# Attention and two expert layers on one core: weighted sums with both halves of V in one product, and what moves with them

## The chip, the cores and the metric

The kernel runs on one core of a Trainium2 chip. Its engines are TensorE (PE), VectorE (DVE), ScalarE (ACT), GpSimd (POOL) and SyncE (SP), which issues the DMAs. Each works through its own instructions in order and waits on semaphores for the others. The metric is the device time of one execution in microseconds (us), the median of several.

## The reference

```python
scores = scale * np.matmul(q, k.transpose(0, 1, 3, 2))          # 4 batches, 8 heads, 576 x 64
kth = np.partition(scores, -32, axis=-1)[..., -32:-31]
scores = np.where(scores >= kth, scores, -1e9)
attn = np.exp(scores - np.max(scores, axis=-1, keepdims=True))
attn = attn / (np.sum(attn, axis=-1, keepdims=True) + 1e-09)
x = (attn @ v) as (2304, 512)
h = x @ w_in                                                     # 512 -> 1024
solu = h * softmax(h)
ln = (solu - mean) / np.sqrt(var + 1e-06) * g_ln
x2 = ln @ w_out                                                  # 1024 -> 512
h = x2 @ w_in2                                                   # 512 -> 2048
out = (h * (1 / (1 + np.exp(-1.702 * h)))) @ w_out2              # 2048 -> 512
```

All of it is float32.

## The kernel before

Products are made in half precision, with each operand as a high half and a low half (`split`): the high half is the number rounded, the low half the rest, and a product is three products, high by high, high by low and low by high. `split` is used for keys, queries, values and weights. In its most frequent form ScalarE scales the raw tile, then squares it with the sum kept (`total`), then writes the high half, and GpSimd writes the low half; the Square writes its unneeded values into the tile of the high half.

**Attention.** Queries are taken in blocks of 128 rows; the last 64 rows of a batch form a block of last rows (`r == NEWT`). A block has four steps (two for last rows), each with two heads: 72 steps. A step goes through TensorE scores (L455), ScalarE copy, VectorE `fold` (L473, L474) and top-k rounds (L484, L487), GpSimd `pick`, ScalarE and GpSimd `mask` (L505), ScalarE `exp_of`, whose accumulator gives the row sums `rsum`, the two halves `high` and `low` (L523), and a DMA transpose `turn` (L528). Three steps behind, `back` (L606) multiplies the transposed weights `et` by V and sums up in the PSUM tile `av`, one bank, of which there is one. For each head and each of five chunks of keys there are three products of 64 columns. When a block is complete, `finish` calls `evac_main` (or `evac_tail`): `recip` (L628, L629) makes the reciprocals of the row sums, and L644 (or L668) multiplies `av` by them into `x`.

**The expert layers.** Each block of 128 rows of `x` then goes through `Block`: `a` (L709), `top`, `e1`, `solu`, `z_high`, `z_low`, `b` (L776), then four times `c` (L806), `tanh`, `gelu` (L815), `g_high`, `g_low` (L826), `d` (L833), and `store`. Its parts are placed between the parts of the attention steps by `at`, some steps later. Weights are decoded from their 64-bit form on VectorE (L249 to L254) and split in the first steps.

**The check at the end.** The program keeps sums of squares, picks and, in `ysum`, the row sums of each stored `y`. At the end VectorE compares them with bounds (`inside`, L1110 to L1113), a product with ones (L1129) adds up the rows, and the flag (L1131) is loaded by every engine; if it is set, a slower version of the whole computation follows.

**What sets the order.** The code is written in the order of the steps, and a scheduler reorders it at build time by priorities and its own estimate. Each engine's order is fixed after that.

Of the kernel before, what the change touches and what calls it, by code (L numbers as in the profile page):

```python
# [41 lines left out]
W_CHECK = 60  # L42
PIN_TO = -1
# [5 lines left out]
S_X2 = 2.0 ** 6  # L49
# [31 lines left out]
def layers(ctx, tc, quick, q, k, v, w1, w2, g_ln, w3, w4, out):  # L81
# [24 lines left out]
    if quick:  # L106
# [5 lines left out]
        ysum = cst.tile([128, NBLK], F32, name="ysum")  # L112
        for i, x in enumerate((1.0, -S_EXP, BIG)):
            nc.vector.memset(pickc[:, :, i], x)
        ones = cst.tile([128, 128], F32, name="ones")
# [4 lines left out]
    def split(raw, hi, lo, scale, what, total=None):  # L120

        n = lo_n[what] = lo_n.get(what, -1) + 1
        how = LO[what][n % len(LO[what])]
# [20 lines left out]
    one = ctx.enter_context(tc.tile_pool(name="one", bufs=1))  # L144
    ep = ctx.enter_context(tc.tile_pool(name="ep", bufs=R_BUFS if quick else 2))
# [43 lines left out]
    nc.vector.memset(mhalf, -0.5)  # L189
    wraw = {}  # L190
# [433 lines left out]
    xm = {}  # L624

    def recip(r, n):

        nc.vector.scalar_tensor_tensor(r[:, 0:n], r[:, 0:n], 1e-9, r[:, 0:n], op0=ALU.add, op1=ALU.max)  # L628
        nc.vector.reciprocal(r, r)  # L629

    def evac_main(blk):
        b, r = blk
        if r == 0:
            batch_coef(b)
        recip(rsum[blk], 8)
        if quick:
            rr = rsum[blk].rearrange("p (a c) -> p a c", c=2)
        else:
            rr = sm.tile([128, 4, 2], F32, tag="rr", name="rr")
            iv = bsc[b][:, 1, 1, :]  # L640
            nc.vector.scalar_tensor_tensor(rr, rsum[blk].rearrange("p (a c) -> p a c", c=2), bcf[b][:, 1:2],
                                           iv[:, :, None].to_broadcast([128, 4, 2]), op0=ALU.mult, op1=ALU.mult)
# [5 lines left out]
        return x, None if quick else bcf[b][:, 2:3]  # L648

    def evac_tail(blk):  # L650
# [5 lines left out]
        if b not in bcf:  # L656
            batch_coef(b)
        rs = rsum[blk][:, 0:4]
        recip(rs, 4)
        rr = rs.rearrange("p (a c) -> p a c", c=2) if quick else sm.tile([128, 2, 2], F32, tag="rrt", name="rrt")  # L660
        for z in range(0 if quick else 2):
            rows = slice(64 * z, 64 * z + 64)
            iv = bsc[b][rows, 1, 1, z::2]
            nc.vector.scalar_tensor_tensor(rr[rows], rs[rows].rearrange("p (a c) -> p a c", c=2),
                                           bcf[b][rows, 1:2], iv[:, :, None].to_broadcast([64, 2, 2]),
                                           op0=ALU.mult, op1=ALU.mult)
        xt = one.tile([128, 512], F32, tag="x", name="xtl")[:, 0:256].rearrange("p (h d) -> p h d", d=64)
        nc.vector.tensor_tensor(xt, pav[blk][:, 0:256].rearrange("p (h d) -> p h d", d=64),  # L668
                                rr.rearrange("p a c -> p (a c)")[:, :, None].to_broadcast([128, 4, 64]),
                                op=ALU.mult)  # L670
# [25 lines left out]
    class Block:  # L696
# [121 lines left out]
        def g_high(self, g):  # L818
# [3 lines left out]
            act(gh[:, 0], t.rearrange("p (a n) -> p a n", a=4))  # L822
# [13 lines left out]
        def store(self):  # L836
            y = at.tile([128, 512], F32, tag="t", name="y")
            if quick:
# [324 lines left out]
```

## Time and profile before

| | |
|---|---|
| median of 3 timed runs | 961.12 us (960.68 to 962.55) |
| the profiled execution, its own time | 967.89 us |
| its span | 966.0 us |
| TensorE busy | 766.2 us (79%) |
| VectorE busy | 766.7 us (79%) |
| ScalarE busy | 722.9 us (75%) |
| GpSimd busy | 695.9 us (72%) |

The span is from the first to the last instruction of the profiled execution; its own time is 1.9 us longer. Busy time is a share of the whole span; stretches differ, and a table by stretches shows them apart. In rows, PE is TensorE, PEld its weight loads, DVE VectorE, ACT ScalarE, POOL GpSimd and SPq the DMA issues of SyncE. L160 is the line of a helper through which all ScalarE operations go.

### The profile page before, as it was taken

What the parts mean: (1) busy time and instruction counts of PE and PEld (TensorE: products, weight loads), DVE (VectorE), ACT (ScalarE), POOL (GpSimd) and SP (SyncE); (2) the same over time, 40 slices, a digit from 0 to 9 for tenths busy, and PEclk for the clock granted to TensorE, in tenths of its full rate; (3) what the DMA queues carried; (4) which work ended last, traced back from release to release, by engine and by line L of the source; (5) the groups of instructions that cost most, each with busy time, mean ns of one, the idle gap of its engine ahead of it and who ended that gap; (6) DMA issues with size and microseconds to landing.
All of it is one profiled execution on the core that took longest, in us unless ns stands there. A gap on an engine that the chain in (4) does not pass through costs nothing.

```text
span 966.0 us, 22236 instructions
## 1 busy us (share of the span) xinstructions
PE 766.2 (79%) x8228; PEld 497.6 (52%) x8228; DVE 766.7 (79%) x2150; ACT 722.9 (75%) x1257; POOL 695.9 (72%) x699
## 2 busy tenths in 40 slices
PE   1122524566688899989999899898999899999996
PEld 0011211534355556656665666565665666666564
DVE  4999999988698999897889988887988899511221
ACT  4689898587888978778899877778997878834431
POOL 2488999778968788777899886777987777733311
PEclk9995756677899999999999999998999899999998
DMA  6998666556757767566778577568756745532200
GB/s 159 314 308 202 178 164 151 122 117 126 143 122 139 122 119 136 105 119 124 137 138 156 115 127 118 100 111 150 137 113 116 130 76 90 97 69 45 44 14 25
DMA packets 337733, 122.66 MB, mean 127 GB/s; under 512 B 315344, under 2 KB 329168, under 8 KB 337616
## 3 DMA queue, kind: packets, MB, share of 16 engines
q1 hardware_dynamic: 337616, 121.16, 61.7%
q8 instruction: 66, 1.08, 0.5%
q14 instruction: 51, 0.42, 0.1%
HBM read 39.85 MB, written 4.72 MB: 46 GB/s over the span
## 4 chain that ended last, share of the span: by engine, by line
PE 26%; ACT 16%; DVE 16%; DMA 15%; POOL 14%; issue 8%; SPq 4%; ACTq 0%; POOLq 0%; DVEq 0%
PE h L806 9%; PE o L833 7%; ACT s L160 4%; PE x L776 4%; DVE wk L484 4%; POOL eh L523 4%; DVE wk L487 4%; PE ha L709 3%; POOL s L505 3%; POOL wt L138 2%; PE sc L455 2%; DMA kt<-kq 2%; ACT kq L160 2%; DMA qt<-kq 2%; DMA et<-eh 2%
## 5 line engine op out<-in xcount | busy, mean ns | idle before, releaser
L484 DVE MAX8 wk<-wk 128x8 f32<-128x296 f32 x576 | 242.2, 461 | 0.0
L806 PE MATMUL h<-x2t,wt 128*128 128x128 f16 x3456 | 217.1, 225 | 20.1 <-DVE t L815 14.8
L806 PEld LDWEIGHTS <-wt 128*128 128x128 f16 x3456 | 206.8, 101 | 27.2 <-issue 15.7
L833 PE MATMUL o<-wt,gh 128*128 128x512 f16 x864 | 203.3, 385 | 9.7 <-DVE wt L254 7.6
L523 POOL TENSOR_TENSOR eh<-s,eh 128x576 f16<-128x576 f32 x144 | 181.5, 1283 | 38.8 <-ACT eh L160 26.2
L505 POOL TENSOR_TENSOR s<-s,r 128x576 f32<-128x576 f32 x144 | 181.8, 1283 | 34.7 <-ACT r L160 34.5
L487 DVE MATCH_REPLACE8 wk<-wk 128x296 f32<-128x296 f32 x432 | 193.6, 458 | 0.0
L455 PE MATMUL sc<-kt,qt 128*128 128x64 f16 (+7 forms) x640 | 99.3, 321 | 71.7 <-DMA qt<-kq 30.8
L606 PE MATMUL av<-vt,et 128*128 128x64 f16 (+1 forms) x2400 | 90.1, 201 | 60.7 <-DMA et<-eh 52.2
L833 PEld LDWEIGHTS <-gh 128*128 128x128 f16 x864 | 83.8, 99 | 105.0 <-issue 16.1
L826 POOL TENSOR_TENSOR gh<-t,gh 128x512 f16<-128x512 f32 x72 | 83.6, 1161 | 73.2 <-ACT gh L160 73.1
L160 ACT ACTIVATE s<-s,picks 128x576 f32<-128x576 f32 x144 | 110.4, 768 | 16.9 <-POOL s L505 16.5
L606 PEld LDWEIGHTS <-et 128*128 128x128 f16 (+1 forms) x2400 | 82.2, 106 | 72.9 <-DMA et<-eh 55.9
L776 PE MATMUL x<-wt,zt 128*128 128x512 f16 x432 | 105.4, 397 | 14.3 <-DMA zt<-zh 14.2
L709 PE MATMUL ha<-wt,xt 128*128 128x512 f16 x432 | 101.9, 394 | 14.5 <-DMA xt<-xhl 11.1
L455 PEld LDWEIGHTS <-qt 128*128 128x128 f16 (+1 forms) x640 | 49.5, 110 | 123.5 <-DMA qt<-kq 31.2
L815 DVE SCALAR_TENSOR_TENSOR t<-t,h 128x512 f32<-128x512 f32 x72 | 49.2, 683 | 76.3 <-ACT t L160 73.3
L160 ACT ACTIVATE r<-s,picks 128x576 bf16<-128x576 f32 x144 | 103.5, 766 | 5.5 <-POOL picks L497 5.4
L160 ACT ACTIVATE t<-h 128x512 f32<-128x512 f32 x72 | 42.3, 588 | 70.7 <-PE h L806 61.9
L160 ACT ACTIVATE s<-sc 128x1152 f32<-128x1152 f32 x72 | 80.7, 1120 | 14.5 <-PE sc L455 8.5
L160 ACT ACTIVATE wt<-wt 128x512 f16<-128x512 f32 (+1 forms) x115 | 68.0, 627 | 22.9 <-DVE wt L254 10.5
L160 ACT ACTIVATE eh<-s 128x1152 f16<-128x1152 f32 x72 | 83.3, 1156 | 0.7
(84 smaller groups left out, 1070.1 us busy)
## 6 DMA issues: line engine op xcount, KB each, us to landing
wt<-in_moe_w_in_dram SPq DMA_DIRECT2D x24, 512.0 KB, 4.8
wt<-in_moe_w_out_dram SPq DMA_DIRECT2D x24, 512.0 KB, 5.7
qt<-qt SPq DMA_DIRECT2D x72, 64.0 KB, 2.0
raw<-in_k_dram SPq DMA_DIRECT2D x32, 128.0 KB, 2.5
raw<-in_q_dram SPq DMA_DIRECT2D x16, 256.0 KB, 3.3
vraw<-in_v_dram SPq DMA_DIRECT2D x32, 128.0 KB, 2.4
out_dram<-y SPq DMA_DIRECT2D x16, 256.0 KB, 3.2
et<-eh SPq DMA_TRANSPOSE x72, 4.7
```

The source lines that it names most:

```text
L160: nc.scalar.activation(out, in_, func, **kw)
L455: nc.tensor.matmul(sc[rows, i * S + c0:i * S + c1], t[qi // 4][:, hl, qi % 4, rows], kts[kp][:, k0 + c0:k0 + c1], start=(hl == 0), stop=(h ...
L484: nc.vector.max(out=wk[:, i, at_:at_ + 8], in_=wk[:, i, 0:W_END])
L487: nc.vector.match_replace(out=wk[:, i, 0:W_END], in_to_replace=wk[:, i, at_:at_ + 8], in_values=wk[:, i, 0:W_END], imm_value=LOW)
L505: nc.gpsimd.tensor_tensor(s[:, i], s[:, i], r[i], op=ALU.subtract)
L523: nc.gpsimd.tensor_tensor(eh[:, 1, cols], s[:, i], eh[:, 0, cols], op=ALU.subtract)
L606: nc.tensor.matmul(o[rows, col:col + 64], et[:, ea, 4 * i + c, rows], vts[kp][:, va, vc:vc + 64], start=(n == 0), stop=(n == 14))
L709: nc.tensor.matmul(h[:, half * 512:half * 512 + 512], self.xt[:, a, kc], w1v(kc, w, half), start=(n == 0), stop=(n == 11))
L776: nc.tensor.matmul(self.x2, self.zt[:, a, kc], w2v(kc, w), start=(n == 0), stop=(n == 23))
L806: nc.tensor.matmul(h2[:, mm * 128:(mm + 1) * 128], w3v(kc, w, 4 * g + mm), self.x2t[:, a, kc], start=(n == 0), stop=(n == 11))
L826: nc.gpsimd.tensor_tensor(gh[:, 1], t.rearrange("p (a n) -> p a n", a=4), gh[:, 0], op=ALU.subtract)
L833: nc.tensor.matmul(self.o, gh[:, a, mm], w4v(4 * g + mm, w), start=(g == 0 and n == 0), stop=(g == 3 and n == 11))
```

## The change

`back` takes both halves of V as one moving operand: for each chunk the high half of the weights is multiplied by 128 columns (V's high half and, 640 elements further, its low half), and the low half of the weights by 64 columns, added to the first 64. Four heads of 128 columns fill the bank, so after every second step `weighted` takes the sums out: the row sums get 1e-9 on GpSimd, VectorE makes the reciprocals and multiplies the two halves apart (L657, L659), and GpSimd adds them (L660). `x` has a pool of its own. In `split` the Square is written behind the halves and into a tile of its own; one Square of a single column stands at the start. The load of `gl` is issued after the first loads. For the last block the check takes, in place of the sums of `y`, the sums of the gelu tile's high half (`accum_out` in `g_high`) and its maximum, and `y` is stored without a sum.

```diff
@@ split
         if how == "A" and scale is not None:
             act(raw, raw, AF.Copy, scale=scale)
-            if total is not None:
-                act(hi, raw, AF.Square, scale=1.0 / scale, accum_out=total)
+            back = 1.0 / scale if total is not None else 1.0
             scale = None
-        elif total is not None:
-            act(hi, raw, AF.Square, accum_out=total)
...
+        if total is not None:
+            junk = squares[:, 0:raw.shape[1] * raw.shape[2]].rearrange("p (c d) -> p c d", d=raw.shape[2]) if len(raw.shape) == 3 \
+                else squares[:, 0:raw.shape[1]]
+            act(junk, raw, AF.Square, scale=back, accum_out=total)
         return how
...
     nc.vector.memset(mhalf, -0.5)
+    if quick:
+        act(squares[:, 0:1], mhalf, AF.Square)
@@ back
-        if j == 0:
+        if j == 0 or quick and j == 2:
             pav[blk] = p_av.tile([128, 512], F32, tag="av", name="av")
         o = pav[blk]
+        for i in range(2 if quick else 0):
+            hs = heads(blk, j, i)
+            col = hs[0][1] % 4 * 128
+            for c in range(5):
+                for ea in range(2):
+                    for rows, qi, kp, par in hs:
+                        vc = par * 320 + c * 64
+                        to = o[rows, col:col + 128 - 64 * ea].rearrange("p (a d) -> p a d", d=64)
+                        nc.tensor.matmul(to, et[:, ea, 4 * i + c, rows], vts[kp][:, 0:2 - ea, vc:vc + 64],
+                                         start=(c == 0 and ea == 0), stop=(c == 4 and ea == 1))
+        if quick:
+            if j % 2:
+                weighted(blk, j // 2)
+            return
...
+    def weighted(blk, half):
+
+        if half == 0:
+            xs[blk] = xp.tile([128, 512], F32, tag="x", name="x")
+        x = xs[blk][:, 256 * half:256 * half + 256].rearrange("p (h d) -> p h d", d=64)
+        r = rsum[blk][:, 4 * half:4 * half + 4]
+        recip(r, 4)
+        o = pav[blk].rearrange("p (h a d) -> p h a d", a=2, d=64)
+        nc.vector.tensor_tensor(x, o[:, :, 0], r[:, :, None].to_broadcast([128, 4, 64]), op=ALU.mult)
+        low = at.tile([128, 4, 64], F32, tag="wl", name="wl")
+        nc.vector.tensor_tensor(low, o[:, :, 1], r[:, :, None].to_broadcast([128, 4, 64]), op=ALU.mult)
+        nc.gpsimd.tensor_tensor(x, x, low, op=ALU.add)
+
     def recip(r, n):
 
-        nc.vector.scalar_tensor_tensor(r[:, 0:n], r[:, 0:n], 1e-9, r[:, 0:n], op0=ALU.add, op1=ALU.max)
+        nc.gpsimd.tensor_scalar(r[:, 0:n], r[:, 0:n], 1.0, 1e-9, op0=ALU.mult, op1=ALU.add)
         nc.vector.reciprocal(r, r)
@@ evac_main
+        if quick:
+            return xs.pop(blk), None
@@ g_high
-            act(gh[:, 0], t.rearrange("p (a n) -> p a n", a=4))
+            if quick and self.no == NBLK - 1:
+                act(gh[:, 0], t.rearrange("p (a n) -> p a n", a=4), accum_out=glast[:, 0, g:g + 1])
+                nc.vector.tensor_reduce(glast[:, 1, g:g + 1], t, axis=AX.X, op=ALU.max)
+            else:
+                act(gh[:, 0], t.rearrange("p (a n) -> p a n", a=4))
...
     gate = last_t[0]
+    load_gl()
     load_for(0)
@@ the check
-    nc.vector.tensor_reduce(ok[:, 5:6], ok[:, 0:5], axis=AX.X, op=ALU.min)
-    bad = sm.tile([128, 1], F32, tag="bad", name="bad")
-    nc.vector.tensor_scalar(bad, ok[:, 5:6], 0.5, None, op0=ALU.is_lt)
+    nc.vector.tensor_scalar(ok[:, 5:9], glast[:, 0], 1e30, None, op0=ALU.is_le)
+    nc.vector.scalar_tensor_tensor(ok[:, 5:9], glast[:, 1], 65000.0, ok[:, 5:9], op0=ALU.is_le, op1=ALU.mult)
+    nc.vector.tensor_reduce(ok[:, 9:10], ok[:, 0:9], axis=AX.X, op=ALU.min)
```

Lines move: scores are L463 after the change, `fold` L481 and L482, the rounds L492 and L495, `back` L614, ScalarE's helper L166.

The order of VectorE around the first block of last rows, before (from its fold to the operation that takes the sums out, `xtl<-av,rsum`):

```order
L473 TENSOR_TENSOR wk<-sc,s 128x2x288
L474 TENSOR_TENSOR sc<-sc,s 128x2x288
L487 MATCH_REPLACE wk<-wk 128x296 x2
L726 TENSOR_SCALAR st<-st 128x1
L253 SCALAR_TENSOR_TENSOR wi<-wt,wi 128x512
L254 SCALAR_TENSOR_TENSOR wt<-wt,wi 128x512
L476 MAX wk<-sc 128x8 x2
L484 MAX wk<-wk 128x8 x2
L728 RECIPROCAL st<-st 128x1
L668 TENSOR_TENSOR xtl<-av,rsum 128x256
```

And with the change:

```order
L481 TENSOR_TENSOR wk<-sc,s 128x2x288
L482 TENSOR_TENSOR sc<-sc,s 128x2x288
L755 TENSOR_SCALAR st<-st 128x1
L492 MAX wk<-wk 128x8
L657 TENSOR_TENSOR x<-av,rsum 128x256
L659 TENSOR_TENSOR wl<-av,rsum 128x256
```

The sums are taken out three rows behind the second folding operation, ahead of the weight decoding and the further rounds; before, they stood behind these.

The order of ScalarE at the start of the program, before (`kq` is the tile of halves, `insq` and `qsq` hold the sums of squares):

```order
L1158 UNCONDITIONAL_BRANCH
L160 ACT_TABLE_LOAD
L160 ACTIVATE kq,insq<-raw 128x10x64
L160 ACTIVATE kq<-raw 128x10x64
L160 ACTIVATE kq,qsq<-raw 128x8x64
L160 ACTIVATE kq<-raw 128x8x64
L160 ACTIVATE wt<-wt 128x512 x3
L160 ACTIVATE kq,insq<-raw 128x10x64
```

And with the change:

```order
L1205 UNCONDITIONAL_BRANCH
L166 ACT_TABLE_LOAD
L166 ACTIVATE squares<-mhalf 128x1
L166 ACTIVATE kq<-raw 128x10x64
L166 ACTIVATE squares,insq<-raw 128x640
L166 ACTIVATE kq<-raw 128x8x64
L166 ACTIVATE squares,qsq<-raw 128x512
L166 ACTIVATE wt<-wt 128x512 x6
```

The table load has a Square of a constant behind it instead of one of the keys, and each Square of keys or queries stands behind the high half.

The order of VectorE at the end, before (`rows` is the product L1129 with ones):

```order
L815 SCALAR_TENSOR_TENSOR t<-t,h_13275 128x512
L815 SCALAR_TENSOR_TENSOR t<-t,h_13346 128x512
L1110 TENSOR_SCALAR junkc<-ysum 128x18
L1111 SCALAR_TENSOR_TENSOR junkc<-ysum,junkc 128x18
L1113 TENSOR_REDUCE ok<-junkc 128x1
L1125 TENSOR_REDUCE ok<-ok 128x1
L1127 TENSOR_SCALAR bad<-ok 128x1
L1131 TENSOR_SCALAR flag<-rows 128x1
L58 TENSOR_LOAD flag
L59 COMPARE_AND_BRANCH
```

And with the change:

```order
L1158 SCALAR_TENSOR_TENSOR junkc<-ysum,junkc 128x17
L1160 TENSOR_REDUCE ok<-junkc 128x1
L853 SCALAR_TENSOR_TENSOR t<-t,h_12655 128x512
L862 TENSOR_REDUCE glast<-t 128x1
L853 SCALAR_TENSOR_TENSOR t<-t,h_12727 128x512
L862 TENSOR_REDUCE glast<-t 128x1
L1172 TENSOR_SCALAR ok<-glast 128x4
L1173 SCALAR_TENSOR_TENSOR ok<-glast,ok 128x4
L1174 TENSOR_REDUCE ok<-ok 128x1
L1178 TENSOR_SCALAR flag<-rows 128x1
L59 TENSOR_LOAD flag
```

The comparison with `ysum` moved ahead of the last two gelu tiles, and behind each of these now stands the maximum of its tile (L862). On TensorE the product for the flag (L1176) stands ahead of the last four products of `d`; before, it stood behind them.

## Rows read from the trace of the kernel before

**Rows 1.** The page: span, busy time of engines, chain by engine and line.

```profile
span 966.0 us, 22236 instructions
...
PE 766.2 (79%) x8228; PEld 497.6 (52%) x8228; DVE 766.7 (79%) x2150; ACT 722.9 (75%) x1257; POOL 695.9 (72%) x699
...
PE 26%; ACT 16%; DVE 16%; DMA 15%; POOL 14%; issue 8%; SPq 4%; ACTq 0%; POOLq 0%; DVEq 0%
PE h L806 9%; PE o L833 7%; ACT s L160 4%; PE x L776 4%; DVE wk L484 4%; POOL eh L523 4%; DVE wk L487 4%; PE ha L709 3%; POOL s L505 3%; POOL wt L138 2%; PE sc L455 2%; DMA kt<-kq 2%; ACT kq L160 2%; DMA qt<-kq 2%; DMA et<-eh 2%
```

**Rows 2.** Stretch, length, busy us of PE, PEld, DVE, ACT, POOL; granted clock, DMA.

```profile
120.00:160.00 40.00, 14.81 (x141) 8.03 (x142) 39.26 (x108) 35.61 (x63) 39.83 (x39) 0.57 0.65 161
320.00:360.00 40.00, 37.08 (x446) 23.21 (x447) 38.86 (x118) 32.30 (x56) 31.55 (x32) 0.96 0.64 120
560.00:600.00 40.00, 40.00 (x445) 26.34 (x444) 36.85 (x109) 29.55 (x53) 27.98 (x27) 1.00 0.78 123
```

**Rows 3.** Order of time around 195 us: start, length, engine, line, operation.

```profile
193.83 1.89 PE L806 MATMUL h<-x2t,wt 128*128 128x128 f16 x31 [0.18 <-DVE t L815]
...
195.56 1.04 PE L606 MATMUL av<-vt,et 128*128 128x64 f16 x30
```

**Rows 4.** Groups of instructions by line: busy us, mean ns; then idle before.

```profile
L806 PEld LDWEIGHTS <-wt 128*128 128x128 f16 x3456 | 206.8, 101 | 27.2 <-issue 15.7 <-DMA x2t<-x2hl 4.3 <-DVE t L815 0.9
...
L606 PE MATMUL av<-vt,et 128*128 128x64 f16 (+1 forms) x2400 | 90.1, 201 | 60.7 <-DMA et<-eh 52.2 <-ACT vt L160 5.1 <-POOL vt L138 3.1
...
L628 DVE SCALAR_TENSOR_TENSOR rsum<-rsum 128x8 f32<-128x8 f32 (+1 forms) x20 | 13.9, 696 | 2.9 <-ACT s L160 2.8
...
L644 DVE TENSOR_TENSOR x<-av,rsum 128x512 f32<-128x512 f32 x16 | 11.0, 688 | 3.0 <-PE av L606 2.9
...
L629 DVE RECIPROCAL rsum<-rsum 128x8 f32<-128x8 f32 (+1 forms) x20 | 3.7, 185 | 0.1
...
L668 DVE TENSOR_TENSOR xtl<-av,rsum 128x256 f32<-128x256 f32 x4 | 1.7, 417 | 0.0
```

**Rows 5.** The same for GpSimd, shapes kept apart.

```profile
L746 POOL TENSOR_SCALAR st<-zsq 128x1 f32<-128x1 f32 x18 | 3.5, 192 | 21.5 <-ACT zh L160 20.6
L138 POOL TENSOR_TENSOR kq<-raw,kq 128x256 f16<-128x256 f32 x4 | 2.7, 674 | 2.5 <-ACT kq L160 2.1 <-DMA vraw<-in_v_dram 0.4
```

**Rows 6.** Order of time from 169 to 178 us, VectorE and GpSimd.

```profile
169.37 8.21 DVE L628 SCALAR_TENSOR_TENSOR rsum<-rsum 128x8 f32<-128x8 f32 x1
...
170.33 2.53 POOL L523 TENSOR_TENSOR eh<-s,eh 128x576 f16<-128x576 f32 x2
...
176.38 1.17 POOL L138 TENSOR_TENSOR wt<-wt 128x512 f16<-128x512 f32 x1
...
177.50 0.68 DVE L253 SCALAR_TENSOR_TENSOR wi<-wt,wi 128x512 int32<-128x512 int32 x1
```

**Rows 7.** Order of time from 124 to 130 us.

```profile
124.64 0.76 DVE L473 TENSOR_TENSOR wk<-sc,s 128x576 f32<-128x576 f32 x1 [0.39 <-POOL picks L497]
...
127.71 1.81 PE L606 MATMUL av<-vt,et 128*64 128x64 f16 x60 [8.59 <-DMA et<-eh]
```

**Rows 8.** The line L644 until 300 us: min, median, max ns; starts.

```profile
L644 DVE TENSOR_TENSOR x<-av,rsum x4: 680/682/693, 98.8 to 280.7; 128x512 f32<-128x512 f32 x4
```

**Rows 9.** Order of time from the start to 11 us.

```profile
0.73 0.46 SPq L908 DMA_DIRECT2D gl<-in_moe_g_ln_dram  x1
...
5.30 1.28 ACT L160 ACT_TABLE_LOAD   x1 [5.30 <-DMA raw<-in_k_dram]
...
6.60 0.74 ACT L160 ACTIVATE kq<-raw 128x640 f16<-128x640 f32 x1
...
10.71 2.65 SPq L411 DMA_TRANSPOSE qt<-kq  x2
```

**Rows 10.** Order of time at the end.

```profile
951.50 5.34 PE L833 MATMUL o<-wt,gh 128*128 128x512 f16 x24
...
959.11 0.16 DVE L1131 TENSOR_SCALAR flag<-rows 128x1 int32<-128x1 f32 x1 [0.47 <-PE rows L1129]
```

More of the change, by code (lines that the diff above doesn't have):

```diff
@@ L42 @@
 W_CHECK = 60
+X_BUFS = 1
 PIN_TO = -1
@@ L111, in layers @@
         zsq = cst.tile([128, NBLK], F32, name="zsq")
-        ysum = cst.tile([128, NBLK], F32, name="ysum")
+        ysum = cst.tile([128, NBLK - 1], F32, name="ysum")
         for i, x in enumerate((1.0, -S_EXP, BIG)):
             nc.vector.memset(pickc[:, :, i], x)
+        squares = cst.tile([128, 640], F16, name="squares")
+        glast = cst.tile([128, 2, 4], F32, name="glast")
         ones = cst.tile([128, 128], F32, name="ones")
@@ L122, in split @@
         n = lo_n[what] = lo_n.get(what, -1) + 1
+        back = 1.0
         how = LO[what][n % len(LO[what])]
@@ L635, in evac_main @@
         recip(rsum[blk], 8)
[L636 to L642, printed above, removed]
+        rr = sm.tile([128, 4, 2], F32, tag="rr", name="rr")
+        iv = bsc[b][:, 1, 1, :]
+        nc.vector.scalar_tensor_tensor(rr, rsum[blk].rearrange("p (a c) -> p a c", c=2), bcf[b][:, 1:2],
+                                       iv[:, :, None].to_broadcast([128, 4, 2]), op0=ALU.mult, op1=ALU.mult)
         x = one.tile([128, 512], F32, tag="x", name="x")
@@ L655, in evac_tail @@
         x, cf = xm[b // 2]
[L656 to L670, printed above, removed]
+        if quick:
+            xt = xs.pop(blk)[:, 0:256].rearrange("p (h d) -> p h d", d=64)
+        else:
+            if b not in bcf:
+                batch_coef(b)
+            rs = rsum[blk][:, 0:4]
+            recip(rs, 4)
+            rr = sm.tile([128, 2, 2], F32, tag="rrt", name="rrt")
+            for z in range(2):
+                rows = slice(64 * z, 64 * z + 64)
+                iv = bsc[b][rows, 1, 1, z::2]
+                nc.vector.scalar_tensor_tensor(rr[rows], rs[rows].rearrange("p (a c) -> p a c", c=2),
+                                               bcf[b][rows, 1:2], iv[:, :, None].to_broadcast([64, 2, 2]),
+                                               op0=ALU.mult, op1=ALU.mult)
+            xt = one.tile([128, 512], F32, tag="x", name="xtl")[:, 0:256].rearrange("p (h d) -> p h d", d=64)
+            nc.vector.tensor_tensor(xt, pav[blk][:, 0:256].rearrange("p (h d) -> p h d", d=64),
+                                    rr.rearrange("p a c -> p (a c)")[:, :, None].to_broadcast([128, 4, 64]),
+                                    op=ALU.mult)
         o = slice(64 * (b % 2), 64 * (b % 2) + 64)
@@ L837, in store @@
             y = at.tile([128, 512], F32, tag="t", name="y")
-            if quick:
+            if quick and self.no < NBLK - 1:
                 act(y, self.o, AF.Copy, scale=0.5 / (S_X2 * S_W[2] * S_W[3]), accum_out=ysum[:, self.no:self.no + 1])
+            elif quick:
+                act(y, self.o, AF.Copy, scale=0.5 / (S_X2 * S_W[2] * S_W[3]))
             else:
@@ L1102, in layers @@
             break
-    ok = sm.tile([128, 6], F32, tag="ok", name="ok")
+    ok = sm.tile([128, 10], F32, tag="ok", name="ok")
     def inside(x, lo, hi, dst):
@@ L1116, in layers @@
     nc.vector.scalar_tensor_tensor(short, picks[:, :, 2], -1.0 / BIG, picks[:, :, 0], op0=ALU.mult, op1=ALU.add)
-    junkc = one.tile([128, short.shape[1]], F32, tag="x", name="junkc")
+    junkc = xp.tile([128, 512], F32, tag="x", name="junkc")[:, 0:short.shape[1]]
     tot = p_av.tile([128, 512], F32, tag="av", name="tot")[:, 0:insq.shape[1]]
@@ L1124, in layers @@
     inside(ysum, -1e30, 1e30, ok[:, 4:5])
-    nc.vector.tensor_reduce(ok[:, 5:6], ok[:, 0:5], axis=AX.X, op=ALU.min)
-    bad = sm.tile([128, 1], F32, tag="bad", name="bad")
-    nc.vector.tensor_scalar(bad, ok[:, 5:6], 0.5, None, op0=ALU.is_lt)
+    nc.vector.tensor_scalar(ok[:, 5:9], glast[:, 0], 1e30, None, op0=ALU.is_le)
+    nc.vector.scalar_tensor_tensor(ok[:, 5:9], glast[:, 1], 65000.0, ok[:, 5:9], op0=ALU.is_le, op1=ALU.mult)
+    nc.vector.tensor_reduce(ok[:, 9:10], ok[:, 0:9], axis=AX.X, op=ALU.min)
     rows = p_av.tile([128, 512], F32, tag="av", name="rows")[:, 0:1]
-    nc.tensor.matmul(rows, ones, bad, start=True, stop=True)
+    nc.tensor.matmul(rows, ones, ok[:, 9:10], start=True, stop=True)
     flag = sm.tile([128, 1], I32, tag="flag", name="flag")
-    nc.vector.tensor_scalar(flag, rows, 0.5, None, op0=ALU.is_gt)
+    nc.vector.tensor_scalar(flag, rows, 127.5, None, op0=ALU.is_lt)
     return flag[0:1, 0:1]
```

13 lines of the change are left out of this document (9 added, 4 removed).

## The prediction

> **What bounds the kernel now.** I read the page first: TensorE and VectorE are busy 79% of the 966.0 us each, and the chain of work that ended last is spread over five: 26% TensorE, 16% ScalarE, 16% VectorE, 15% transfers, 14% GpSimd [rows 1]. No engine alone sets the time, so a change is worth what it does to the engine that ends last in its stretch. The table by stretches shows which: at 120 to 160 us VectorE (39.26 of 40) and GpSimd (39.83) are full and TensorE holds 14.81, mostly at its lower clock; at 320 to 360 us VectorE (38.86) and TensorE (37.08) share it, and at 560 to 600 us TensorE has 40.00 of 40 at full clock [rows 2]. The reader is to see two kernels in one: an early one that ends on VectorE and GpSimd, and a later one that ends mostly on TensorE. From the page's shares I take a price for added work where nothing better is known: of VectorE's 79% a share of 16% is on the chain, so about one us in five; of GpSimd's 72% it is 14%, also one in five; of TensorE's 79% it is 26%, one in three.
>
> **The products.** For each pair of heads, 30 products of 64 columns become 10 of 128 and 10 of 64: 1,920 columns before, 1,920 after. What counts is the spacing of products in a run. At full clock 30 products of L606 span 1.04 us and 31 of L806 (128 columns) 1.89 us [rows 3]; taking off 0.20, the mean record of one [rows 4], that is 29.0 ns and 56.3 ns apart. So 30 x 29.0 = 870 ns become 10 x 56.3 + 10 x 29.0 = 853: 17 ns, times 72 steps 1.2 us. The third of the instructions that goes is worth almost nothing, because columns set the pace. Bounds: 0 (if the moving operand in two pieces, which no row shows, costs as much as two products) to -1.2; a third of it, -0.4. What speaks for more is that a weight load's record lasts longer than that spacing (101 ns in L806 [rows 4]); but they overlap, or 31 pairs would not fit in 1.89 us. The Trainium skill, "TensorE: Matmul & The Clock Gate", section "Back-to-back issue gap", gives a sustained spacing of about 81 ns for 128 columns in streams of load and product, and keeps the 56 ns for a single product. The trace disagrees (56.3 in a run of 31 pairs); by the page the step would take 1,100 ns, 17 us more in all.
>
> **Taking the sums out.** Before, a block of four steps had one operation of 512 elements (688 ns, x16), one of last rows had one of 256 (417, x4), 12.7 us, and there were 20 reciprocals of 185 ns, 3.7 us [rows 4]. Now there are 36 sets, each of two operations of 256 elements from PSUM (2 x 417) and a reciprocal: 36 x 1.019 = 36.7 us. VectorE gets +20.3 us; a fifth, +4.1 (bounds 0 and +20.3). GpSimd gets per set an addition of 256 elements (674 ns by the row of that size that writes half precision) and the row-sum operation (192 ns by a one-column one) [rows 5]: 36 x 0.866 = 31.2 us; a fifth, +6.1 (0 to +31.2). What hides the rest is TensorE in the later stretches; before 300 us that cover is missing, and the same work would cost nearly all of it.
>
> **The row sums.** L628 leaves VectorE. Its 20 instances take 13.9 us [rows 4], of which one takes 8.21: it starts at 169.37, while GpSimd's operations on SBUF follow each other, and ends at 177.58, within 0.03 us of the end of the last of these (176.38 + 1.17) [rows 6]. It has both inputs in SBUF, and I read it as held off by GpSimd. The new VectorE operations have one input in SBUF, as L644 and L668 have, whose means of 688 and 417 ns hide no such stretch. So up to 8.0 us go. I take -6: GpSimd was full just before [rows 2], and part of what it did in that time would have been waited for anyway. The bounds are -8.0 and 0, the latter if the timed runs do not meet that moment: the profiled execution took 967.89 us, 6.8 above the median of 961.12, which is about the size of this one wait. The other 19 hold 2.7 us above 0.16 each; a fifth, -0.5.
>
> **A new wait.** The sums are now taken out as soon as the products are issued. VectorE's order shows it for the first block of last rows: L657 stands four rows behind its fold, where L668 stood nine behind. In the trace that fold starts at 124.64 and lasts 0.76, so behind a second one of its kind and two short ones L657 would come up at about 126.6, while the products run from 127.71 for 1.81 us [rows 7]: VectorE stands still some 2.9 us. Behind it wait the weight decoding (L262, then ScalarE) and the top-k rounds; on GpSimd the addition L660 now waits for VectorE, with masks and low halves behind it. Four blocks and one of last rows are taken out before 300 us, the fourth at 280.7 [rows 8], so nine sets; at half of 2.9 each that is 13 us, a fifth +2.6 (0 to +26). Before the second set of a block TensorE has to wait until the bank is emptied, too; in nearly all steps it has other products queued between.
>
> **Squares, start, end.** The Square that sums up inputs wrote the tile that the high half needs; now it comes after. Nothing leaves ScalarE, but the half is there 0.74 us earlier (first instance [rows 9]). Over the span "ACT kq", the Squares and high halves of keys and queries, holds 2% of the chain [rows 1], 19 us, about half of it Squares; less the start, which comes next, some 8. Each place where the chain is freed has other work close behind, so I take half: -4 (0 to -8). At the start three things leave the way to the first scores: the load of gl ahead of the keys (0.46), the table load (1.28, now issued before any input is there) and this Square (0.74): -2.5 on the transposes that were issued at 10.71 [rows 9]; bounds -1, if the reordered key loads take it back before the second scores, and -2.9. At the end the flag no longer waits for the last y. Before, it came at 959.11 + 0.16, behind 24 products that end at 956.84 and, after them, y and five operations on VectorE [rows 10]. Now the check needs the last gelu tile, and its product stands ahead of the last four products; after y only the store is left: -2.4 (-1.8 to -2.9). The last block's four maxima on VectorE lie under TensorE's products.
>
> **The sum.** -0.4 + 4.1 + 6.1 - 6 - 0.5 + 2.6 - 4 - 2.5 - 2.4 = -3.0 us against the profiled 967.89, so 964.9; on the median of the timed runs 958.1, in round numbers 958. That is the forecast, slightly faster.
>
> **The rivals.** *Hidden both ways* (no change): with half of the 6 us not there in the timed runs the sum is 0, and small costs decide: 959.2 to 963. *VectorE waits for the weighted sums* (slower): if the early waits count in full instead of a fifth, 13 for 2.6, the sum is +7.4, 968.5; with 2.9 at each of the nine, +20.4, 981.5. It decides once L657's waits for the sums pass 6 us in all before 300 us; before, L644 waited 2.9 over the whole span [rows 4]. For it: both engines are full there; against: VectorE gets the time of its removed wait. *The wide product is spaced by its load* (slower): at 101 ns a step would take 1,300 ns, +0.43 x 72 = +31 us, a third on the path: +7.7 in all, 968.8, at most 989.5. The run of 31 speaks against it. By the 81 ns of the Trainium skill's page named above, the addition would be about half of that. *The gains count whole* (much faster): -8.0 - 2.7 - 8 - 2.9 - 2.9 - 1.2 with 10.2 of added work is -15.5, 945.6; for it speaks that the long wait stands on the chain, and that the order of the steps behind is nearly the same as before, so that early time saved would be saved at the end.
>
> **How the numbers follow.** Forecast (951 to 959.2) 0.38; whole gains (943 to 951) 0.12; hidden 0.22; VectorE waits (963 to 975, or more) 0.24; wide products slow 0.04. A change of 0.2% is 1.9 us, about what a measurement of this kernel can tell from none. So faster 0.50, same 0.22, slower 0.28. Leaving out half of the whole gains and the upper part of the slower cases gives 946 to 968; the forecast's own range is 951 to 959.
>
> **What would show it.** Right: runs of the weighted sums still near 0.85 us and a record at full clock; no VectorE operation of several us beside GpSimd work; VectorE busy some 6 us more and GpSimd some 31; first qt transposes issued near 8.2 us; the flag there before the last y. Wrong: waits at L657 over 6 us, L660 late with the masks behind it, TensorE standing between the two sets, or a first fold no earlier than before. If early time saved is lost again before the stretch that TensorE fills, the forecast becomes "no change".

## The result, and the profile after

The changed kernel takes 966.71 us (median of 7 runs, 965.23 to 968.92), the kernel before 961.74 in the same session: a ratio of 1.0056, 95% interval 1.0041 to 1.0072. It is slower by about 5 us, where slightly faster was forecast. The profiled executions of the kernel before (967.89, and 969.32 in a second one) lie above its timed runs, so all verdicts below are ratios of timed runs; 0.001 is about 1 us.

The page of the changed kernel, to set beside [rows 1]: span, busy time, chain by engine.

```profile
span 965.2 us, 20776 instructions
...
PE 758.8 (79%) x7428; PEld 493.2 (51%) x7428; DVE 771.6 (80%) x2203; ACT 720.9 (75%) x1261; POOL 727.6 (75%) x771
...
PE 20%; POOL 20%; DVE 17%; ACT 15%; DMA 14%; issue 8%; SPq 5%; POOLq 0%; ACTq 0%; DVEq 0%
```

GpSimd got 31.7 us more (31.2 forecast), VectorE 4.9 more (some 6) and TensorE 7.4 less, and GpSimd's share of the chain went from 14% to 20%. The stretches of [rows 2], in the same columns:

```profile
120.00:160.00 40.00, 11.58 (x110) 7.40 (x108) 38.09 (x101) 32.34 (x56) 37.77 (x38) 0.55 0.60 146
320.00:360.00 40.00, 36.49 (x389) 22.89 (x390) 36.84 (x113) 31.89 (x54) 34.80 (x37) 0.96 0.64 116
560.00:600.00 40.00, 38.81 (x407) 25.75 (x404) 38.95 (x122) 31.65 (x53) 32.97 (x36) 1.00 0.67 107
```

VectorE is nearly as full as before in the first two and fuller in the third, and TensorE no longer fills 560 to 600 us. The operations that came, by line (busy us, mean ns, then idle before), and one run of the wide products (start, length):

```profile
L660 POOL TENSOR_TENSOR x<-x,wl 128x256 f32<-128x256 f32 x36 | 26.2, 729 | 10.4 <-DVE wl L659 10.1
...
L659 DVE TENSOR_TENSOR wl<-av,rsum 128x256 f32<-128x256 f32 x36 | 14.9, 413 | 0.0
L657 DVE TENSOR_TENSOR x<-av,rsum 128x256 f32<-128x256 f32 x36 | 14.8, 410 | 8.4 <-PE av L614 8.3
...
L664 POOL TENSOR_SCALAR rsum<-rsum 128x4 f32<-128x4 f32 x36 | 7.0, 194 | 13.7 <-ACT s L166 11.3
...
L665 DVE RECIPROCAL rsum<-rsum 128x4 f32<-128x4 f32 x36 | 6.0, 167 | 11.0 <-POOL rsum L664 10.8
```

```profile
285.03 1.01 PE L614 MATMUL av<-vt,et 128*128 128x128 f16 x20
```

The sizes are as forecast: a set costs VectorE 0.41 + 0.41 + 0.17 us and GpSimd 0.73 + 0.19, and 20 products take 1.01 us where 30 took 1.04 [rows 3]. VectorE's wait for the products until 300 us and, below it, four of its waits over the whole span (total, times, longest):

```profile
DVE x L657 <- PE av L614: 2.5, 3, 1.4
```

```profile
DVE wk L481 <- ACT s L166: 28.6, 23, 6.8
DVE x2hl L830 <- ACT x2hl L166: 19.8, 10, 5.0
...
DVE rsum L665 <- POOL rsum L664: 10.8, 11, 2.5
DVE x L657 <- PE av L614: 8.3, 6, 3.6
```

The start and the end, in order of time, to set beside [rows 9] and [rows 10]:

```profile
8.22 4.32 SPq L419 DMA_TRANSPOSE qt<-kq  x2
...
13.41 0.61 PE L463 MATMUL sc<-kt,qt 128*128 128x512 f16 x1 [13.41 <-DMA qt<-kq]
...
18.97 0.76 DVE L481 TENSOR_TENSOR wk<-sc,s 128x576 f32<-128x576 f32 x1 [6.79 <-ACT s L166]
```

```profile
953.52 4.48 PE L875 MATMUL o<-wt,gh 128*128 128x512 f16 x20
...
957.84 0.28 PE L1176 MATMUL rows<-ok,ones 128*128 128x1 f32 x2
...
957.98 1.02 PE L875 MATMUL o<-wt,gh 128*128 128x512 f16 x4
958.15 0.16 DVE L1178 TENSOR_SCALAR flag<-rows 128x1 int32<-128x1 f32 x1 [0.85 <-PE rows L1176]
```

The second folding step, before and then with the change:

```profile
26.00 0.75 DVE L473 TENSOR_TENSOR wk<-sc,s 128x576 f32<-128x576 f32 x1
```

```profile
30.93 0.76 DVE L481 TENSOR_TENSOR wk<-sc,s 128x576 f32<-128x576 f32 x1
```

The transposes of the queries are issued 2.5 us earlier, at 8.22, but their record is 4.32 us long in place of 2.65, and the first products come at 13.41 (13.47 before). The first fold starts no earlier (18.97, before 18.96), and the second 4.9 us later. One load of keys that was issued ahead of the transposes is now issued behind them, at 15.89 us. At the end the flag is there while the last four products still run; from the last product's end to the span's end are 6.2 us, 9.2 before. So the products, the row sums and the end did what they were said to do and the start did not; by the fifth fold (66.1 us, before 66.2) its delay is made up, so most of the time is lost behind it.

### The profile page after: what moved, and what is told of

It is laid out like the page before. It is cut to its first block, busy times and chain, and to the rows that moved or that the text cites. A ratio compares the mean times of both kernels' runs of the same rounds, so it can differ in the third digit from the quotient of the medians.

```text
span 965.2 us, 20776 instructions
## 1 busy us (share of the span) xinstructions
PE 758.8 (79%) x7428; PEld 493.2 (51%) x7428; DVE 771.6 (80%) x2203; ACT 720.9 (75%) x1261; POOL 727.6 (75%) x771
## 4 chain that ended last, share of the span: by engine, by line
PE 20%; POOL 20%; DVE 17%; ACT 15%; DMA 14%; issue 8%; SPq 5%; POOLq 0%; ACTq 0%; DVEq 0%
PE h L844 6%; PE o L875 6%; POOL eh L531 5%; ACT s L166 4%; DVE wk L492 4%; PE x L814 4%; POOL s L513 4%; DVE wk L495 4%; PE ha L747 3%; DMA raw<-in_k_dram 2%; DMA raw<-in_q_dram 2%; POOL gh L868 2%; DMA et<-eh 2%; POOL wt L139 2%; DMA vraw<-in_v_dram 2%
## 5 line engine op out<-in xcount | busy, mean ns | idle before, releaser
L492 DVE MAX8 wk<-wk 128x8 f32<-128x296 f32 x576 | 240.0, 454 | 0.0
L495 DVE MATCH_REPLACE8 wk<-wk 128x296 f32<-128x296 f32 x432 | 191.8, 449 | 0.0
L463 PE MATMUL sc<-kt,qt 128*128 128x64 f16 (+7 forms) x640 | 98.2, 324 | 83.8 <-DVE wk L484 40.4
L614 PE MATMUL av<-vt,et 128*128 128x128 f16 (+2 forms) x1600 | 89.5, 221 | 87.5 <-DMA et<-eh 70.6
L614 PEld LDWEIGHTS <-et 128*128 128x128 f16 (+1 forms) x1600 | 78.4, 109 | 105.1 <-DMA et<-eh 93.3
L166 ACT ACTIVATE s<-s,picks 128x576 f32<-128x576 f32 x144 | 110.2, 766 | 14.8 <-POOL s L513 14.3
L166 ACT ACTIVATE r<-s,picks 128x576 bf16<-128x576 f32 x144 | 103.2, 764 | 19.4 <-POOL picks L505 19.4
L463 PEld LDWEIGHTS <-qt 128*128 128x128 f16 (+1 forms) x640 | 49.1, 111 | 132.2 <-issue 37.1
L814 PE MATMUL x<-wt,zt 128*128 128x512 f16 x432 | 101.2, 386 | 7.3 <-DMA zt<-zh 6.6
L747 PE MATMUL ha<-wt,xt 128*128 128x512 f16 x432 | 98.3, 383 | 1.3 <-DVE x2hl L830 1.3
L166 ACT ACTIVATE s<-sc 128x1152 f32<-128x1152 f32 x72 | 80.5, 1118 | 18.8 <-PE sc L463 15.1
L166 ACT ACTIVATE t<-h 128x512 f32<-128x512 f32 x72 | 42.2, 585 | 56.0 <-PE h L844 51.3
L166 ACT ACTIVATE eh<-s 128x1152 f16<-128x1152 f32 x72 | 83.2, 1155 | 0.9 <-DMA et<-eh 0.2
L166 ACT ACTIVATE wt<-wt 128x512 f16<-128x512 f32 (+1 forms) x115 | 67.4, 626 | 15.6 <-DVE wt L262 6.5
```

Of the source, the lines that this page charges most:

```text
L166: nc.scalar.activation(out, in_, func, **kw)
L463: nc.tensor.matmul(sc[rows, i * S + c0:i * S + c1], t[qi // 4][:, hl, qi % 4, rows], kts[kp][:, k0 + c0:k0 + c1], start=(hl == 0), stop=(h ...
L492: nc.vector.max(out=wk[:, i, at_:at_ + 8], in_=wk[:, i, 0:W_END])
L495: nc.vector.match_replace(out=wk[:, i, 0:W_END], in_to_replace=wk[:, i, at_:at_ + 8], in_values=wk[:, i, 0:W_END], imm_value=LOW)
L614: nc.tensor.matmul(to, et[:, ea, 4 * i + c, rows], vts[kp][:, 0:2 - ea, vc:vc + 64], start=(c == 0 and ea == 0), stop=(c == 4 and ea == 1))
L747: nc.tensor.matmul(h[:, half * 512:half * 512 + 512], self.xt[:, a, kc], w1v(kc, w, half), start=(n == 0), stop=(n == 11))
```

## The experiments

Every edit makes the scheduler order all engines anew. Between the changed kernel and the same with the old start (a4 below), 457 of VectorE's 1,748 instructions and 337 of ScalarE's 930 that both have stand elsewhere among the others. So there are two kinds of runs: edits in the order that the scheduler makes for them, and edits in an order held fixed, by a list of places that was read off another build:

```python
for e, row in PINNED.items():          # instructions of one engine, in the wanted order
    for a, b in zip(row, row[1:]):
        tc.add_manual_dep(b, a.name, mybir.DependencyInfo(mybir.DependencyClass.NoSync,
                                                          mybir.DependencyReason.DATA), reason="in_order")
```

An instruction that the other build lacks stands behind the one that it follows in the code. Line numbers rise by 29 in such kernels. Holding an order costs nothing that shows: d1 below holds the kernel before with one operation exchanged, and takes the same time. The changed kernel was not run with its own order held and nothing else altered.

| run | wide products | row sums on | start | end | order | us | ratio to before, 95% |
|---|---|---|---|---|---|---|---|
| before | no | VectorE | old | old | own | 962 | 1 |
| changed | yes | GpSimd | new | new | own | 966.7 | 1.0056 (1.0041 to 1.0072) |
| a2 | no | GpSimd | new | new | own | 956.7 | 0.9945 (0.9921 to 0.9969) |
| a3 | yes | VectorE | new | new | own | 973.5 | 1.0131 (1.0088 to 1.0174) |
| a4 | yes | GpSimd | old | new | own | 957.3 | 0.9935 (0.9913 to 0.9957) |
| b1 | no | GpSimd | old | old | own | 955.7 | 0.9944 (0.9925 to 0.9964) |
| b2 | no | GpSimd | old | new | own | 953.2 | 0.9924 (0.9893 to 0.9954) |
| b3 | yes | GpSimd | gl alone new | new | own | 967.3 | 1.0074 (1.0050 to 1.0097) |
| b4 | yes | VectorE | old | old | own | 960.6 | 0.9997 (0.9978 to 1.0016) |
| c1 | yes | GpSimd | new | new | of a4 | 955.2 | 0.9935 (0.9911 to 0.9958) |
| c2 | yes | GpSimd | old | new | of changed | 974.1 | 1.0125 (1.0097 to 1.0154) |
| d1 | no | VectorE, one input | old | old | of before | 962.9 | 1.0000 (0.9984 to 1.0017) |
| d2 | yes | GpSimd | old | new | of b2 | 969.0 | 1.0065 (1.0042 to 1.0089) |
| d3 | no | GpSimd | new | new | of b2 | 955.9 | 0.9930 (0.9907 to 0.9952) |
| d4 | yes | GpSimd | new | new | of d2 | 966.0 | 1.0036 (1.0016 to 1.0056) |
| e1 | no | GpSimd | old | old | of before | 954.8 | 0.9922 (0.9895 to 0.9948) |
| e2 | no | VectorE | old | old | of b1 | 965.2 | 1.0015 (0.9997 to 1.0034) |

In d2 and d4 `x` has two buffers, in the changed kernel one. Differences in us between two runs are differences of their ratios, times 962; with the intervals of both, one of less than about 3 us is not clear of noise.

**Which part costs the time?** First the kernel before once more, and three runs that each undo one part (a2 takes `back`, `evac_main` and `evac_tail` as they were, without `weighted`):

```diff
# a3
-        nc.gpsimd.tensor_scalar(r[:, 0:n], r[:, 0:n], 1.0, 1e-9, op0=ALU.mult, op1=ALU.add)
+        nc.vector.scalar_tensor_tensor(r[:, 0:n], r[:, 0:n], 1e-9, r[:, 0:n], op0=ALU.add, op1=ALU.max)
# a4; b3 the same, but with load_gl() left where the change put it
-        act(squares[:, 0:1], mhalf, AF.Square)
+            act(hi, raw, AF.Square, accum_out=total)
             act(hi, raw)
-            act(junk, raw, AF.Square, scale=back, accum_out=total)
# a4 alone: the load of gl is issued ahead of the keys again
```

> The kernel before, unchanged, to see whether its profile of 967.89 us is its usual course. Theory (the 8.21 us of the row-sum operation at 169 us is an accident of that execution, and the predicted -6 us was never there to gain): a time of 959 to 963 us, and no row-sum operation over 2 us. Rival (the wait belongs to the program): an operation of several us again near 169 us, and a profiled time near 967.

> The changed kernel with the weighted sums as before (products of 64 columns, one taking out for a block); the row sums stay on GpSimd, the start and the end stay changed. Theory GpSimd and VectorE pay for the second half (36 additions of 729 ns on GpSimd, some 20 us on VectorE): 957 to 960 us, faster than before by 2 to 4. Rival the start (reordered key loads, first scores 4 us later): still 964 to 967. Rival row sums on GpSimd: still 964 to 967 too; the next two runs tell these two apart.

> The changed kernel with the row-sum operation back on VectorE as before (both inputs in SBUF); wide products, start and end stay changed. Theory GpSimd's queue (its row-sum operation waits for ScalarE 11 us in all and VectorE's reciprocal waits for it 11 us): 962 to 964. Rival wide products cost the time: 965 to 968, no better, or worse by a long VectorE operation.

> The changed kernel with the start as before: the Squares ahead of the halves, no early table load, gl loaded ahead of the keys. Wide products, row sums on GpSimd and the new end stay. Theory the start loses what it was to gain (the second scores 4 us later): 962 to 964 us, second scores back at 21.3 us. Rival the start does nothing for the end, as the time is lost on GpSimd between 238 and 390 us: 966 to 968.

The second profile of before took 969.32 and holds the long row-sum operation again (line, then min, median and max ns):

```profile
L628 DVE SCALAR_TENSOR_TENSOR rsum<-rsum x20: 147/158/7970, 87.8 to 842.6; 128x8 f32<-128x8 f32 x16, 128x4 f32<-128x4 f32 x4
```

By the ratios, undoing the wide products alone gives back 10.7 us and undoing the start alone 11.6, more than the change lost in all, so the two don't add up (a4's 957.3 us lies below what both its theory and its rival said). Putting the row sums back costs 7.2 more. So parts were next made alone:

> The kernel before with one line changed: the row-sum operation moves from VectorE to GpSimd. The unchanged kernel showed the long row-sum operation again (7.97 us at 169 us), so it belongs to the program. Theory (the wait was worth the predicted 6 us and reaches the end): 955 to 958 us. Rival (time saved at 170 us is lost again before TensorE's stretch): 960 to 963, folds some 8 us earlier at 184 us and level again by 390 us.

> Row sums on GpSimd and the new end, with narrow products and the start as before. Theory (terms add up: row sums -5, end -2.5): 953 to 956 us. Rival (the changed kernel with narrow products took 956.7 and that with the old start 957.3; if the two costs are one and the same scheduling accident): 956 to 958, no better than either.

> The changed kernel, but with the Squares ahead of the high halves again and no early table load; gl stays behind the keys. In the order of the transfers the fourth key load is then back ahead of the first transposes. Theory (the moved Square sends that key load behind the transposes, and that is the start's whole cost): 956 to 960 us, second fold at 26 us. Rival (gl's place costs it): 965 to 967.

> The kernel before with the wide products and the two sets alone; row sums stay on VectorE, start and end as before. Theory (the wide products with their second half cost 8 to 10 us by themselves, as between the changed kernel and its run with narrow products): 970 to 973 us. Rival (they cost 10 only beside the late start): 962 to 966.

The row sums alone win 5.4 us (b1), and with the end 7.3 (b2), the fastest kernel in the scheduler's own orders. With the wide products alone the time stays (b4, below both ranges given for it). That does not make them free: in b4's order the long row-sum operation is gone, too,

```profile
L660 DVE SCALAR_TENSOR_TENSOR rsum<-rsum x36: 140/162/1275, 58.6 to 838.8; 128x4 f32<-128x4 f32 x36
```

with 1.28 us at most, so b4 shows their cost less whatever that gave back. The theory on the start fell: b3 differs from a4 only in where one small load, gl, is issued, its key loads are back in their old order and its second fold comes at 25.4 us, and it is as slow as the changed kernel. One moved load makes 13 us by the ratios. What moved with it are the places of some 470 of VectorE's instructions. Whether the load or the places cost the time, c1 tells: it has gl there, too.

**Order or work?** So the same work was run in two orders:

```diff
+    if quick:
+        pinned(tc, start)      # c1: the changed kernel, PINNED = order of a4; c2: a4, PINNED = order of the changed kernel
```

> The changed kernel, all of its work, with each engine's order held fixed: the order that the scheduler chose for the changed kernel with the old start (957.3 us), with each Square behind its high half and gl's load a little later. Theory order (the scheduler's new order of everything behind costs the 9 us between those two kernels, not the work at the start): 955 to 959 us. Rival work (the moved Squares and gl themselves cost it): 964 to 968.

> The other way round: the changed kernel with the old start, each engine held in the order that the changed kernel has (966.7 us), each Square ahead of its high half and gl first. Theory order: 964 to 969 us. Rival work: 956 to 959.

Order it is, and not gl's place. In the traces the lists were kept: c1 has VectorE's instructions in a4's order but for one of 2,203, and c2 in that of the changed kernel but for one. The whole change in a4's order takes 955.2 us, faster than before by 0.65%; in its own order 966.7, 11.6 us more for the same instructions. The old start in the changed kernel's order is slow too. TensorE's clock over a whole execution doesn't explain it: the granted clock was 0.931 to 0.954 in the seven timed runs of the changed kernel and 0.928 to 0.950 in the seven of c1. The page of c1 has a shorter span with nearly the same busy times, but for TensorE's (11.4 us less):

```profile
span 952.5 us, 20798 instructions
...
PE 747.4 (78%) x7428; PEld 485.7 (51%) x7428; DVE 772.1 (81%) x2203; ACT 720.8 (76%) x1261; POOL 727.3 (76%) x771
```

Where c1 gains shows in two stretches (length, then busy us and instructions of PE, PEld, DVE, ACT, POOL; granted clock; DMA), first the changed kernel, then c1:

```profile
160.00:280.00 120.00, 83.11 (x718) 55.09 (x719) 107.22 (x303) 96.02 (x167) 108.62 (x113) 0.82 0.68 141
280.00:540.00 260.00, 235.17 (x2357) 152.39 (x2355) 223.45 (x670) 208.57 (x366) 214.43 (x232) 0.96 0.64 121
```

```profile
160.00:280.00 120.00, 77.69 (x644) 47.77 (x644) 103.06 (x290) 91.74 (x160) 102.74 (x106) 0.80 0.64 132
280.00:540.00 260.00, 238.94 (x2486) 157.76 (x2486) 234.07 (x703) 216.98 (x378) 225.89 (x244) 0.98 0.72 130
```

c1 is behind at first (it has done fewer instructions by 280 us; its sixteenth fold starts at 230.2 against 221.8), and its VectorE even stands 5.0 us at the start for the moved gl. From 280 to 540 us it does 703 instructions on VectorE against 670, with TensorE's clock at 0.98 against 0.96, and its last fold starts at 816.1 against 828.1. VectorE's waits in c1, line for line with those of the changed kernel above:

```profile
DVE wk L510 <- ACT s L195: 24.6, 21, 5.2
...
DVE x2hl L859 <- ACT x2hl L195: 13.3, 6, 5.7
DVE rsum L694 <- POOL rsum L693: 7.9, 8, 3.9
...
DVE x L686 <- PE av L643: 4.8, 6, 1.7
```

These four waits fall from 67.5 to 50.6 us; all the time that VectorE is not busy (span less busy) falls by 13.2, from 193.6 to 180.4, as others grow, gl's among them. What such a wait is, at one place of the changed kernel (order of time, VectorE and ScalarE):

```profile
296.46 0.83 DVE L492 MAX8 wk<-wk 128x8 f32<-128x296 f32 x2
302.26 0.69 DVE L830 SCALAR_TENSOR_TENSOR x2hl<-x,x2hl 128x512 f16<-128x512 f32 x1 [4.98 <-ACT x2hl L166]
304.33 0.76 DVE L481 TENSOR_TENSOR wk<-sc,s 128x576 f32<-128x576 f32 x1 [1.38 <-ACT s L166]
```

```profile
301.63 0.60 ACT L166 ACTIVATE x2hl<-x 128x512 f16<-128x512 f32 x1 [0.24 <-PE x L814]
...
303.18 1.12 ACT L166 ACTIVATE s<-sc 128x1152 f32<-128x1152 f32 x1
```

VectorE reaches L830 at 297.3 and stands until 302.26, since the high half of x2 on ScalarE waits for products that end at 301.6. Behind L830 stands the next fold; its scores had been done since 291.8, but ScalarE's copy of them stands behind x2 too, so the fold starts at 304.33. In c1 the same fold starts at 301.5, after a start 7.9 us later for the fold ahead of it. An engine that works in order waits for what its list says next, not for what is ready.

**What the parts cost when the order is held.** The changed kernel in its own order, with less work in two operations:

```diff
-        nc.gpsimd.tensor_tensor(x, x, low, op=ALU.add)
+        nc.gpsimd.tensor_tensor(x[:, :, 0:1], x[:, :, 0:1], low[:, :, 0:1], op=ALU.add)      # c3
-        nc.vector.tensor_tensor(low, o[:, :, 1], ...)
+        nc.vector.tensor_tensor(low[:, :, 0:1], o[:, :, 1, 0:1], ...)                        # c4, with the line above
```

> The changed kernel with each engine's order held as it is, but GpSimd's addition of the two halves takes one column of 64 (the output leaves out most of the low half of V): some 36 x 0.6 = 21 us of GpSimd work less, everything else in its place. Theory GpSimd (a fifth, as the prediction has it, or more where it is full): 960 to 963 us. Rival order alone (GpSimd's additions are hidden): 965 to 968.

> As the run before, and VectorE's second taking out (the low half) takes one column of 64 too: another 36 x 0.3 = 11 us of VectorE work less (the output leaves out most of the low half). Theory VectorE (a fifth of it or more on the path): 2 to 4 us below the run before. Rival: within 1 us of it.

c3 took 963.7 us, ratio 1.0017 (0.9997 to 1.0036); c4 964.4, 1.0031 (1.0011 to 1.0050). The two operations in them:

```profile
L689 POOL TENSOR_TENSOR x<-x,wl 128x4 f32<-128x4 f32 x36 | 7.5, 208 | 13.8 <-DVE wl L688 13.0 <-DVE rsum L694 0.6
```

```profile
L688 DVE TENSOR_TENSOR wl<-av,rsum 128x4 f32<-128x4 f32 x36 | 5.7, 157 | 0.0
```

36 x (729 - 208) = 18.8 us less on GpSimd give 3.8 us, one in five, though by the intervals it may be anything from 0.1 to a third; the time lies between the ranges of theory and rival. 36 x (413 - 157) = 9.2 us less on VectorE give none that shows. Then the row sums, and the other parts in the order of b2:

```diff
-        nc.vector.scalar_tensor_tensor(r[:, 0:n], r[:, 0:n], 1e-9, r[:, 0:n], op0=ALU.add, op1=ALU.max)
+        nc.vector.tensor_scalar(r[:, 0:n], r[:, 0:n], 1.0, 1e-9, op0=ALU.mult, op1=ALU.add)  # d1
+        nc.gpsimd.tensor_scalar(...)                                                         # e1; e2 the other way
```

> The kernel before, each engine held in the order it has, with one thing changed: the row-sum operation, still on VectorE and in its place, takes one input from SBUF and a constant in place of two inputs from SBUF. Theory (the long operation comes of its two SBUF inputs beside GpSimd's work, and its 8 us reach the end): no row-sum operation over 1 us, and 954 to 958 us. Rival (any VectorE operation at that place would be held): 960 to 964 with the long operation still there. Rival (it goes, but the time is lost again): 959 to 963 without it.

> Wide products and two sets put into the order of the kernel with narrow products, row sums on GpSimd and the new end (953.2 us): every other instruction keeps its place on its engine; the first set of a block is taken out where its products ended in that kernel's trace; x has two buffers. Theory order (the wide products by themselves cost no more than the addition's 3 us): 953 to 957 us. Rival (they cost 5 to 10 in any order): 958 to 963.

> The moved Squares, the early table load and gl behind the keys, put into the order of the same kernel of 953.2 us, with narrow products. Theory (the start's work gains 2 us when the order behind it stays, as between 957.3 and 955.2): 950 to 953 us. Rival (no gain, or a loss): 953 to 957.

> The whole change in that order: wide products and the new start together, with row sums on GpSimd and the new end; x has two buffers. Theory (terms add where the order is held): within 2 us of the sum of the two runs before, 952 to 956 us. Rival (wide products and start cost 9 to 10 us together, as in the scheduler's own orders): 960 to 967.

> The row-sum operation on GpSimd, with every other instruction of the kernel before held in the place that it has there; GpSimd gets it at the moment at which VectorE had started it. Theory (the wait of 8 us was worth its time, as the prediction has it): 954 to 957 us. Rival (the 5.9 us that this edit won in the scheduler's order came from the new order): 960 to 963 us, without any VectorE operation over 1.5 us.

> The other way round: the row-sum operation on VectorE, with two inputs from SBUF, and every other instruction held in the order of the kernel that had it on GpSimd (955.7 us). Theory (the operation's place beside GpSimd costs the time): 960 to 964 us, with an operation of several us again. Rival (order): 954 to 958 us.

d1 changed nothing, because the operation with one input was held as long (order of time, VectorE and GpSimd):

```profile
170.25 8.27 DVE L657 TENSOR_SCALAR rsum<-rsum 128x8 f32<-128x8 f32 x1
...
171.25 2.54 POOL L552 TENSOR_TENSOR eh<-s,eh 128x576 f16<-128x576 f32 x2
...
177.31 1.18 POOL L167 TENSOR_TENSOR wt<-wt 128x512 f16<-128x512 f32 x1
...
178.43 0.68 DVE L282 SCALAR_TENSOR_TENSOR wi<-wt,wi 128x512 int32<-128x512 int32 x1
```

With the operation on GpSimd and every other instruction in its old place (e1), 7.5 us are won; with it back on VectorE in b1's order (e2) 6.8 are lost, and its longest instance is 5.29 us there. So this wait is worth its time in either order. The start costs or wins nothing in b2's order (d3), wins 2.8 in d4 against d2, which is within the noise, and in c2's order 6.6 (the changed kernel against c2). The wide products cost 13.6 in b2's order (d2, more than its rival said), which was made for narrow ones, and 1.1 where the scheduler could order for them (a4 against b2). The whole change in that order of b2 (d4) loses 3.5 us against before: its rival was right, and an order that is held is not by itself a good one.

## Why the prediction was wrong

The direction failed. The measured 966.7 us lies in the range of 946 to 968 and outside the forecast's own, 951 to 959; it is in the range by the part kept for the slower rivals, and neither of their mechanisms is in the trace, so that is luck. Point by point:

- **The products**: right. 20 in 1.01 us; nothing is spaced by weight loads, so that rival fell.
- **Taking the sums out**: sizes right. GpSimd's price of one in five agrees with the 3.8 of 18.8 us, within wide noise; VectorE's +4.1 looks too high, as far as half of its added time shows (none of 9.2 us). The whole of the wide products (products, sums and new wait) was put at +12.4: they cost 13.6 (d2 against b2), 10.7 (the changed kernel against a2) and 1.1 (a4 against b2), by order.
- **The row sums**, -6.5: right in size, 7.5, 6.8 and 7.2 us (e1, e2, a3 against the changed kernel). That GpSimd's work holds it off was right, too; two inputs in SBUF are not needed for it (d1).
- **The new wait**: its first nine sets waited 2.5 us, not 13, and 8.3 in the span; the rival that VectorE waits for the sums asked for 6 before 300 us and fell. A wait that was not forecast came beside it: the reciprocal L665 stands 10.8 us for GpSimd's L664.
- **Start and Squares**, -2.5 and -4: mis-sized, and in b2's order the term furthest off. In a4's order they are worth nothing (c1 against a4, both 0.9935), in b2's nothing or 2.8 (d3 against b2, d4 against d2); only in the changed kernel's order 6.6. The transposes were issued early, as forecast, and landed no earlier; the second fold came 4.9 us later, where the bound for reordered key loads still had a gain of 1.
- **The end**, -2.4: right in the trace. b2 has b1's order and the new end; in its profile the span ends 6.3 us behind the last product, in b1's 9.3. Its time is 1.9 us less, which alone is within the noise.
- **The sum**, -3.0: this is the step that failed. It adds prices as if the instructions behind stayed in their places; the prediction says so only where it argues for whole gains, and calls the order of the steps behind "nearly the same as before, so that early time saved would be saved at the end". Between the changed kernel and a4 about a quarter of VectorE's instructions have other places, and many of the other engines'; the order alone is worth 11.6 us (the changed kernel against c1), 18 in the other pair (c2 against a4). In a4's order the change wins 6.3 us, twice the forecast; in its own it loses 5.4. None of the rivals named this. Nor do the terms come out at -3.0 once an order is held: in b2's the change loses 3.5 (d4), of which row sums and end are -7.3 (-8.9 forecast), the wide products +13.6 (+12.4) and start and Squares -2.8 (-6.5). No run held the whole change in the order of the kernel before itself.

The place at 297 us is an example of how an order costs time. That such places in VectorE's list alone make up the 11.6 us was not shown: no run moved single instructions, and the order of TensorE, ScalarE and GpSimd differs as well.

## What to carry to other kernels

Where a scheduler orders the program anew at each build, an edit has two effects, its own and that of the new order, and here the second was the larger: 11.6 and 18 us against 6.3. Hold the order when an edit is to be priced, by dependencies that follow a list read off the build; then the price of the held row sums came out as computed in two orders, and that of GpSimd's addition within its noise. A held order prices small edits; one that was made for the old work can be bad for new work, as 13.6 us for the wide products in b2's order against 1.1 in one made for them show. And once an edit is good, try it in several orders: the whole change was a loss of 0.56% or of 0.36%, or a gain of 0.65%, with the same operations.

## What the runs showed of the hardware

A VectorE operation on 8 columns in SBUF was held 8.27 us beside a train of seven GpSimd operations, and let go when the train ended; MAX8 and MATCH_REPLACE8, also on SBUF, kept their 0.45 us beside such trains. It was held with two inputs from SBUF (7.97) and with one and a constant (8.27). It is not always held to the end of a train: in a3 one such operation was let go after 0.85 us, at the end of the first of two GpSimd operations that follow each other (VectorE, then GpSimd):

```profile
61.27 0.85 DVE L664 SCALAR_TENSOR_TENSOR rsum<-rsum 128x4 f32<-128x4 f32 x1
```

```profile
60.83 2.52 POOL L531 TENSOR_TENSOR eh<-s,eh 128x576 f16<-128x576 f32 x2 [1.74 <-ACT eh L166]
```

What decides between the two was not found. The Trainium skill, "SBUF — State Buffer", section "Who interferes with whom", names VectorE operations with two SBUF inputs, and `tensor_scalar` in a mode that takes both ports, as ones that contend with GpSimd, and says that the loser is blocked fully. The trace agrees on both operations, though no run shows in which mode d1's ran. The Trainium skill's same page, section "Summary: rules for kernel authors", says until the first finishes; the trace agrees in a3, and in d1 it was seven operations. The reciprocal of the same columns was never held (0.17 us, 36 times), and GpSimd does the operation in 0.19.
